# A fused attention and Fourier-mix kernel: turning the exponentials on TensorE instead of by DMA, and moving one cast in GpSimd's order

## The chip, the cores and the metric

The kernel runs on one core of one Trainium2 chip. The metric is the device time of one execution in microseconds (us); lower is better. Times are medians over several executions, and one execution of each kernel is also recorded by the hardware profiler, with every instruction's start, duration and releaser. The engines are named as the profile names them: PE is TensorE's matmul and PEld its weight load, DVE is VectorE, ACT is ScalarE, POOL is GpSimd and SP is SyncE, which here only issues DMAs.

## The reference

For each of 8 batches, 8 heads of a 512-row input `x` and a 32-row `state` attend to each other in both directions; the two results are joined to 544 rows of 512 columns. A Fourier transform over rows and columns is added (real part), the rows are normalised, and a two-layer network with a relu is added.

```python
scores  = (x @ state^T) / sqrt(64);   xread = softmax(scores)  @ state     # 512 rows per head
scores2 = (state @ x^T) / sqrt(64);   sread = softmax(scores2) @ x         #  32 rows per head
a = concat([xread, sread], rows)      # per batch, heads side by side: 544 x 512
u = a + real(fft(fft(a, rows), columns))
un = (u - mean(u)) / sqrt(var(u) + 1e-6)
out = u + relu(un @ w_ch1) @ w_ch2    # w_ch1: 512 x 2048, w_ch2: 2048 x 512
```

## The kernel before

Everything is written for one core, with the order of the instructions of all five engines set by the order in which the Python code emits them. Nothing is rescheduled: each engine works through its own list from top to bottom and waits where an operand is not there. So the place of a step in the code is its place on every engine that it uses.

**Rows.** The 512 rows of a batch lie in four tiles of 128 partitions. Tile 0 is rows 1 to 128; tile 1 rows 144 to 271; tile 2 rows 273 to 400; tile 3 holds 32 single rows (129 to 143, 0, 401 to 415, 272; these are the "low rows") and rows 416 to 511. The transform uses the symmetry of sines and cosines: rows k and 544 - k are added and subtracted ("folded") before they are multiplied with the tables, so tiles 1 and 3 are needed in reverse row order (`XR`), tiles 0 and 2 in forward order (`XF`).

**Steps of one batch `b`.** `load_x` (L115) brings x into `xs` in float32, eight DMAs from SP; `cast_x` (L139) makes the bf16 copy `xin` on GpSimd, one instruction (L140). `turn_state` and `turn_x` (L367, L378) give the transposed `sT` and `xT`; from batch 2 on they are six DMA transposes issued by SP. `scores` (L419) multiplies them on TensorE and writes the exponentials `E` through ScalarE (L430). `E` must then be turned as well, to `ET`, to serve as weights of `xread` (L453). There are two ways in the code. `turn_scores` (L433) multiplies `E` by an identity, or by `mirror` where a tile must be reversed, on TensorE, and ScalarE copies the product to `ET` and adds up the row `sums` (L438); batch 2 takes this way. From batch `e_by_dma = 3` on, `turn_scores_by_dma` (L441) issues two DMA transposes from SP, and `add_scores` (L444) makes the sums by a ScalarE pass over `ET` (L447). [...] for these batches tiles 1 and 3 must be reversed ahead: `turn_x_in_dram` (L134) copies their rows of `x` in reverse order to `x_dram`, two DMAs from memory to memory, one batch ahead, and `load_x` reads `x_dram` for these two tiles.

**Reading and folding.** `read_low` (L511) runs `xread` for tile 3 (TensorE L462, then VectorE L470 and L471 into `XR`), and GpSimd copies its 32 low rows to `XT` (L513). `fold_low` (L515) adds and subtracts halves of `XT` into `XEl` and `XOl` (L516 to L518), on GpSimd too. `sread` (batches 0 and 1) or `sread_by_head` (later batches) overwrites those low rows of `XR` with sread's result (L490 and L492, or L508). For batch 1 GpSimd then adds up a row tile (L529) and makes `XQl` (L523 to L526). `fold` (L537) does the rest on VectorE.

**Transform and network.** `transform` multiplies with the row tables (L634), then with the column tables (L588, L589); VectorE adds (L593) and takes statistics (L330, L332); `ub` is the centred tile, turned to `unT` (by SP's DMA transposes from batch 2 on, L667). `layer1` multiplies `unT` with `w_ch1` (L763 for batch 0, L753 for others; relu on ScalarE, L765 and L755), and `layer2` multiplies with `w_ch2` (L817), scales and adds on VectorE (L784) and stores (L788, L798, L799).

**The order.** Around the start, a list written out by hand (L856 to L860) interleaves transform and first layer of batch 0 with the turns, scores and reads of batch 1. In that list `last_loads` ends with batch 2's cast, `turned[2]` issues batch 2's six transposes and `load_x3` the loads of batch 3. After it, a loop (L865) weaves the streams of neighbouring batches: second layer of `b - 1`, first layer of `b`, reads and transform of `b + 1`, scores of `b + 2`. `warm` fills TensorE with matmuls whose result is not used. PSUM tiles of `scores`, `turn_scores`, `second_axis` and `over_s` share three banks (`psQ`); those of the layers share three others (`psF`); `x2` has one pair.

Of the kernel before, what the change touches and what calls it, by code (L numbers as in the profile page):

```python
# [12 lines left out]
F32 = mybir.dt.float32  # L13
BF16 = mybir.dt.bfloat16
I32 = mybir.dt.int32
AF = mybir.ActivationFunctionType
# [14 lines left out]
def kernel(  # L31
# [8 lines left out]
    nc = tc.nc  # L40
    B, H, S, D = x.shape
    Ns = state.shape[2]
    dm = H * D
# [7 lines left out]

    r_dram = nc.dram_tensor("r_dram", (B, 2, 128, dm), F32, kind="Internal")
    s_dram = nc.dram_tensor("s_dram", (B, H, Ns, D), F32, kind="Internal")
    x_dram = nc.dram_tensor("x_dram", (B, 224, dm), F32, kind="Internal")
# [58 lines left out]
    e_by_dma = 3  # L113

    def load_x(b):  # L115
        xs = wk.tile([128, 4 * dm], F32, name="xs", tag="xs")
        xs_of[b] = xs
        v = xs.rearrange("p (i h d) -> p i h d", i=4, d=D)
        xb = x[b].rearrange("h s d -> s h d")
        back = [x_dram[b, rows].rearrange("r (h d) -> r h d", d=D) for rows in (slice(0, 128), slice(128, 224))]  # L120
        for ps, si, rows in (
            (slice(0, 128), 0, xb[1:129]),
            (slice(0, 128), 1, xb[144:272] if b < e_by_dma else back[0]),
            (slice(0, 128), 2, xb[273:401]),
            (slice(32, 128), 3, xb[416:512] if b < e_by_dma else back[1]),
            (slice(0, 15), 3, xb[129:144]),
            (slice(16, 31), 3, xb[401:416]),
            (slice(15, 16), 3, xb[0:1]),
            (slice(31, 32), 3, xb[272:273]),
        ):  # L130
            queue = nc.scalar if b == 0 and si in (0, 2) else nc.sync
            queue.dma_start(out=v[ps, si], in_=rows)

    def turn_x_in_dram(b):  # L134
        for rows, top in ((slice(0, 128), 271), (slice(128, 224), 511)):
            n = rows.stop - rows.start
            nc.sync.dma_start(out=x_dram[b, rows].rearrange("r (h d) -> h r d", d=D), in_=x[b, :, top:top - n:-1, :])

    def cast_x(b, copy=nc.gpsimd.tensor_copy, lo=0, hi=4):  # L139
        copy(xin_bufs[b % 2][:, lo:hi, 1:513], xs_of[b].rearrange("p (i c) -> p i c", i=4)[:, lo:hi])  # L140
# [163 lines left out]
    def more_loads():  # L304
        state_blocks(1, 2, nc.gpsimd.tensor_copy)
        nc.gpsimd.tensor_copy(gate[:, 0:1], XQ0[:, 3, 0, 0:1])
        cast_x(1)
        nc.gpsimd.tensor_tensor(gate, xs_of[0][:, 0:4], w1[:, :, 3 * 512], op=ALU.add)
        turn_in_dram(3, B)
        load_x(2)  # L310
        turn_x_in_dram(3)
        clears(1)
        nc.gpsimd.memset(stb[:, 2:].rearrange("p b g c -> p (b g c)").bitcast(F32), 0.0)

    def last_loads():
        nc.gpsimd.tensor_copy(gate[:, 0:1], xs_of[2][:, 0:1])
        for q in range(4):
            nc.gpsimd.dma_start(out=w2[:, q * 4:(q + 1) * 4, :], in_=w2v[:, q * 4:(q + 1) * 4, :])
        state_blocks(2, 3, nc.gpsimd.tensor_copy)
        cast_x(2)  # L320

    def qt(name, dt=F32):
        return psQ.tile([128, 512 if dt == F32 else 1024], dt, name=name, tag="q")
# [29 lines left out]
    def attend(b):  # L353
# [8 lines left out]
        ET = wk.tile([128, 2, S] if b < e_by_dma else [128, 8, 128], BF16, name="ET", tag="ET")  # L362
        E = wk.tile([128, 4, 2, 128], BF16, name="E", tag="E")
        sums = wk.tile([128, 2], F32, name="sums", tag="sums")
        Sm = wk.tile([128, 2, 514], BF16, name="Sm", tag="Sm", bufs=1)
# [72 lines left out]
            nc.scalar.activation(ET[:, g, :], p, AF.Copy, accum_out=sums[:, g:g + 1])  # L438


        def turn_scores_by_dma(i):  # L441
            nc.sync.dma_start_transpose(out=ET[:, 4 * i:4 * i + 4, :], in_=E[:, 2 * i:2 * i + 2].rearrange("p a b c -> p (a b c)"))

        def add_scores():  # L444
            junk = Sm[:, 0, 0:512].rearrange("p (a c) -> p a c", c=128)
            for g in range(2):
                nc.scalar.activation(junk, ET[:, g:8:2, :], AF.Copy, accum_out=sums[:, g:g + 1])  # L447

        def weights_of(g, c0):
            return ET[:, g, c0:c0 + 128] if b < e_by_dma else ET[:, c0 // 64 + g, :]  # L450


        def xread(c0, rev, name, o, ps=slice(0, 128), apart=False):  # L453
            n = ps.stop - ps.start
            p = None if apart else x2(name)
            rs = wk.tile([128, 2, 4], F32, name="rs", tag="rs", bufs=4)
            ov = o.rearrange("p (g h d) -> p g h d", g=2, d=D)
            for half in range(2):
                g = 1 - half if rev else half
                rhs = sb[:, g, 259::-1] if rev else sb[:, g, 4:264]  # L460
                ph = psF.tile([128, 512], F32, name=name, tag="c") if apart else p[:, half]
                nc.tensor.matmul(ph[:, 0:260], lhsT=weights_of(g, c0), rhs=rhs, start=True, stop=True)  # L462
# [8 lines left out]
            nc.vector.tensor_tensor(  # L471
                ov, in0=p[ps, :, 0:256].rearrange("p g (h d) -> p g h d", d=D),
                in1=rs[ps].unsqueeze(3).to_broadcast([n, 2, 4, D]), op=ALU.mult)
# [84 lines left out]
        if b < 2:  # L558
            first = [turn_state, lambda: turn_x(0), lambda: turn_x(1)]
            if b == 1:  # L560
                first = [turn_all] + [lambda i=i: copies[i]() for i in range(3)]
            first += [lambda: scores_t(0), lambda: scores_t(1),
                     lambda: scores(0), lambda: scores(1)]
        else:
            first = [lambda: scores(0), lambda: scores(1), lambda: turn_scores(1), lambda: turn_scores(0)]
            if b >= e_by_dma:
                first = [lambda: (scores(0), turn_scores_by_dma(0)), lambda: (scores(1), turn_scores_by_dma(1)), None, None]
            if b >= x_by_dma:
                turned[b] = lambda: (turn_state(), turn_x(0), turn_x(1))
            else:  # L570
                first = [turn_state, lambda: turn_x(0), lambda: turn_x(1)] + first
        read = lambda c0, rev, o: lambda: xread(c0, rev, "xrp" if rev else "xfp", o, apart=(b == 0 and not rev))
        if b < 2:
            second = [read_low, sread, fold_low, read(0, False, XF[:, 0, 0:512]),
                      lambda: (fold_rows(slice(0, 1), nc.gpsimd), fold_low_again()),
                      read(128, False, XF[:, 1, 0:512]), None,
                      lambda: (read(256, True, XR[:, 1, 1:513])(), fold())]
        else:
            second = [read_low, fold_low, read(0, False, XF[:, 0, 0:512]), lambda: (b >= e_by_dma and add_scores(), sread_by_head()),
                      read(128, False, XF[:, 1, 0:512]), None,  # L580
                      lambda: (read(256, True, XR[:, 1, 1:513])(), fold())]
        return first, second
# [256 lines left out]
    def warmed(steps, n):  # L839
        return [lambda s=s: (s(), warm(n)) for s in steps if s is not None]  # L840
# [5 lines left out]
    for step in warmed(s0[:1], 8) + warmed(s0[1:2], 6) + warmed(s0[2:3], 14) + [second_table] + warmed(s0[3:5], 4) + s0[5:]:  # L846
# [1 line left out]
    sin_table()  # L848
    weave((warmed(r0, 4), 0, 1), ([sines], 0.25, 0.25), ([more_sines], 0.3, 0.3),
          ([lambda: warm(44)], 1, 1))  # L850
    load_x3 = lambda: (load_state(3, B, s_dram), load_x(3), turn_x_in_dram(4))
    scores_next, reads_after = attend(2)
    L, M, r1, t1 = layer1(0), layer2(0), reads_next, transform(1)
    W = lambda n: (lambda: warm(n))
    turns1, copies1, s1 = s1[0], s1[1:4], s1[4:]
    for step in (warmed(t0[:2], 2) + [alternate, more_loads] + warmed(t0[2:4], 2) + [exp_again, last_loads, turned[2], load_x3,  # L856
            t0[4], t0[8], W(6), turns1, t0[5], W(10), t0[7], copies1[0], copies1[1], t0[6], copies1[2],
            L[0], s1[0], t0[9], L[1], t0[10], s1[1], L[2], t0[11], t0[12], L[3], s1[2], r1[0], L[4], s1[3],
            r1[2], t0[13], L[5], r1[1], L[6], r1[3], L[7], r1[4], r1[5], L[8], r1[7],
            lambda: state_ones(2, B), lambda: [r() for r in first_roots], L[9], L[10]]):  # L860
        step()
    weave((L[11:], 0, 0.25), (t1, 0.2, 1), ([M[i] for i in (0, 4, 1, 5, 2, 6, 3, 7, 8, 9)], 0.33, 0.99),
# [2 lines left out]
    for b in range(1, B + 1):  # L865
# [10 lines left out]
            streams.append(([lambda: (cast_x(b + 2), turned[b + 2]())], 0.2, 0.2))  # L876
            streams.append((scores_next, 0.5, 1))
        if b + 3 < B:
            streams.append(([lambda: (load_x(b + 3), b + 4 < B and turn_x_in_dram(b + 4))], 0.35, 0.35))
        if b in (3, 7):  # L880
            streams.append((low_rows(b // 4), 0.02, 0.2))
            streams.append((layer1(("L", b // 4)), 0.36, 0.8))
# [31 lines left out]
```

## Time and profile before

| | us |
|---|---|
| median of three runs | 312.68 |
| lowest and highest run | 311.18, 313.35 |
| the profiled execution, whole | 312.68 |
| its span, first to last instruction | 310.9 |
| TensorE busy | 290.4 |
| VectorE busy | 180.5 |
| ScalarE busy | 140.5 |
| GpSimd busy | 96.7 |

A line of instructions in the profile reads: line of the kernel, engine, operation, output `<-` inputs, shapes, then count, busy time, mean duration, and the idle time of the engine just before with what ended it. In a timeline a line begins with the start in us from the span's start and the duration. Matmuls overlap, so their durations add up to more than the time that passes; the distance of two starts is what one costs. `PEld` lines are weight loads, which run beside matmuls. The throttle granted TensorE 0.998 of its full clock.

The DMAs of the two parts that the change touches, as the profile lists them for the whole execution: `x_dram<-in_x_dram`, five of 256 KB and five of 192 KB; `xs<-x_dram`, the same; `ET<-E`, ten transposes. All were issued by SP, on the queue that moved 32.33 MB of the 38.47 MB.

### The profile page before, as it was taken

What the parts mean: (1) busy time and instruction counts of PE and PEld (TensorE: products, weight loads), DVE (VectorE), ACT (ScalarE), POOL (GpSimd) and SP (SyncE); (2) the same over time, 40 slices, a digit from 0 to 9 for tenths busy, and PEclk for the clock granted to TensorE, in tenths of its full rate; (3) what the DMA queues carried; (4) which work ended last, traced back from release to release, by engine and by line L of the source; (5) the groups of instructions that cost most, each with busy time, mean ns of one, the idle gap of its engine ahead of it and who ended that gap; (6) DMA issues with size and microseconds to landing.
All of it is one profiled execution on the core that took longest, in us unless ns stands there. A gap on an engine that the chain in (4) does not pass through costs nothing.

```text
span 310.9 us, 5979 instructions
## 1 busy us (share of the span) xinstructions
PE 290.4 (93%) x2276; PEld 165.4 (53%) x2276; DVE 180.5 (58%) x433; ACT 140.5 (45%) x267; POOL 96.7 (31%) x217
## 2 busy tenths in 40 slices
PE   5968979999968999999999999999999999999993
PEld 5866967544524554456644454445444544555442
DVE  7786674867766576781926756584759474000021
ACT  5777755646533443435434444435343542334200
POOL 4888574490253022700306022601340131000000
PEclk9999999999999999999999999999999999999999
DMA  7998983764754975346753574254333023500354
GB/s 166 204 193 196 174 154 75 194 141 106 195 122 114 217 153 144 69 110 171 177 118 89 131 191 119 63 124 86 101 84 69 35 75 90 124 28 33 76 135 103
DMA packets 117546, 38.47 MB, mean 124 GB/s; under 512 B 107582, under 2 KB 111934, under 8 KB 117518
## 3 DMA queue, kind: packets, MB, share of 16 engines
q1 hardware_dynamic: 106798, 32.33, 44.0%
q0 software_dynamic: 4224, 4.19, 8.5%
q10 hardware_dynamic: 6496, 1.57, 2.3%
q8 instruction: 18, 0.29, 0.4%
q14 instruction: 10, 0.08, 0.1%
HBM read 24.71 MB, written 16.32 MB: 132 GB/s over the span
## 4 chain that ended last, share of the span: by engine, by line
PE 76%; DVE 6%; POOL 5%; issue 4%; ACT 4%; DMA 3%; SPq 1%; POOLq 0%; DVEq 0%; ACTq 0%
PE po L817 31%; PE ph L753 29%; PE ph L763 3%; PE gp L634 2%; PE warm L837 2%; DVE XF L471 2%; POOL xin L140 1%; PE xrp L462 1%; PE po L809 1%; DVE XR L508 1%; PE yp L589 1%; PE yp L588 1%; ACT Sm L447 1%; PE esp L425 1%; DMA xT<-xin 1%
## 5 line engine op out<-in xcount | busy, mean ns | idle before, releaser
L817 PE MATMUL po<-w,hT 128*128 128x512 bf16 x496 | 124.2, 379 | 0.0
L755 ACT ACTIVATE hT<-ph 128x512 bf16<-128x512 f32 x112 | 66.8, 597 | 119.8 <-PE ph L753 118.2
L753 PE MATMUL ph<-unT,w 128*128 128x512 bf16 x448 | 113.7, 379 | 1.5 <-issue 1.5
L753 PEld LDWEIGHTS <-w 128*128 128x128 bf16 x576 | 50.8, 98 | 49.6 <-issue 2.0
L817 PEld LDWEIGHTS <-hT 128*128 128x128 bf16 x496 | 47.3, 98 | 47.9
L784 DVE SCALAR_TENSOR_TENSOR ot<-po,rstd,U 128x512 f32<-128x512 f32 (+2 forms) x33 | 24.2, 733 | 49.5 <-PE po L817 47.3
L638 POOL COPY GL<-G 128x128 bf16<-128x128 bf16 x8 | 2.3, 293 | 80.0 <-ACT G L635 80.0
L593 DVE TENSOR_TENSOR U<-yp,XR 128x512 f32<-128x512 f32 x16 | 10.9, 683 | 26.7 <-PE yp L589 26.7
L336 POOL TENSOR_TENSOR rstd<-mv,epst 128x1 f32<-128x1 f32 x34 | 7.9, 231 | 47.0 <-DVE mv L332 47.0
L337 POOL TENSOR_TENSOR rstd<-rstd,mhalf 128x1 f32<-128x1 f32 x34 | 21.2, 623 | 2.7
L330 DVE BATCH_NORM_STATS2 st<-U 128x6 f32<-128x512 f32 x32 | 21.8, 682 | 0.1
L635 ACT CAST G<-gp 128x288 bf16<-128x288 f32 x31 | 14.5, 483 | 7.7 <-PE gp L634 7.7
L140 POOL CAST xin<-xs 128x2048 bf16<-128x2048 f32 (+1 forms) x9 | 14.4, 1605 | 7.1 <-PE ph L763 3.7
L763 PE MATMUL ph<-unT,w 128*128 128x128 bf16 x256 | 16.1, 219 | 0.5 <-ACT unT L674 0.5
L837 PE MATMUL warm<-ident 128*128 128x128 bf16 x144 | 12.8, 241 | 3.7 <-POOL ident masks.py:199 3.6
L763 PEld LDWEIGHTS <-w 128*128 128x128 bf16 x256 | 15.0, 98 | 0.8 <-issue 0.6
L837 PEld LDWEIGHTS <-ident 128*128 128x128 bf16 x144 | 10.7, 110 | 4.1 <-POOL ident masks.py:199 3.6
L662 DVE TENSOR_SCALAR ub<-U,mv 128x512 bf16<-128x512 f32 x24 | 12.3, 514 | 0.9
L462 PEld LDWEIGHTS <-ET 128*128 128x128 bf16 x64 | 5.3, 98 | 13.6 <-DVE XF L471 5.0
L513 POOL COPY XT<-XR 32x514 bf16<-32x514 bf16 x8 | 4.8, 604 | 21.9 <-DVE XR L471 21.9
L471 DVE TENSOR_TENSOR XR<-xrp,rs 128x512 bf16<-128x512 f32 x16 | 11.1, 695 | 0.7
L593 DVE TENSOR_TENSOR U<-yp,XF 128x510 f32<-128x510 f32 x16 | 10.8, 674 | 0.0
(189 smaller groups left out, 363.0 us busy)
## 6 DMA issues: line engine op xcount, KB each, us to landing
xs<-in_x_dram SPq DMA_DIRECT2D x17, 256.0 KB
w<-in_moe_w_ch_dram POOLq DMA_DIRECT2D x8, 512.0 KB, 11.1
out_dram<-ot SPq DMA_DIRECT2D x15, 256.0 KB
r_dram<-ot SPq DMA_DIRECT2D x14, 256.0 KB
out_dram<-r_dram SPq DMA_DIRECT2D x14, 256.0 KB
x_dram<-in_x_dram SPq DMA_DIRECT2D x5, 256.0 KB
xs<-x_dram SPq DMA_DIRECT2D x5, 256.0 KB
x_dram<-in_x_dram SPq DMA_DIRECT2D x5, 192.0 KB
```

Of the source, the lines that this page charges most:

```text
L140: copy(xin_bufs[b % 2][:, lo:hi, 1:513], xs_of[b].rearrange("p (i c) -> p i c", i=4)[:, lo:hi])
L330: nc.vector.bn_stats(st6, u)
L337: nc.gpsimd.tensor_tensor(rstd, rstd, mhalf, op=ALU.pow)
L471: nc.vector.tensor_tensor(ov, in0=p[ps, :, 0:256].rearrange("p g (h d) -> p g h d", d=D), in1=rs[ps].unsqueeze(3).to_broadcast([n, 2, 4, D ...
L593: nc.vector.tensor_add(u.rearrange("p (k r) -> p k r", r=2), p.rearrange("p (r k) -> p k r", r=2)[:, 0:u.shape[1] // 2, :], x.rearrange("p ...
L635: (nc.vector.tensor_copy if b == 0 and j == 3 else nc.scalar.copy)(G[:, j, :].rearrange("p (i q) -> p q i", q=2), p[:, 0:NM].rearrange("p ...
L753: nc.tensor.matmul(ph[:, o:o + n], lhsT=w1[:, c, f * 128:(f + 1) * 128], rhs=un_of[key][:, c, :], start=(c == 0), stop=(c == DC - 1))
L755: nc.scalar.activation(hT[:, per * i:per * i + per, :].rearrange("p a b -> p (a b)"), ph, AF.Relu, scale=-1.0 if key in flipped else 1.0)
L763: nc.tensor.matmul(ph[:, o:o + 128], lhsT=w1[:, c, f * 128:(f + 1) * 128], rhs=un_of[key][:, c, 128 * r:128 * r + 128], start=(c == 0), st ...
L784: nc.vector.scalar_tensor_tensor(ot[:, cols], in0=po_of[i][:, 0:cols.stop - cols.start], scalar=rstd, in1=u[:, cols], op0=ALU.mult, op1=AL ...
L817: nc.tensor.matmul(po_of[i], lhsT=h_of[key][:, f, i * 128:(i + 1) * 128], rhs=w2[:, f, :], start=(f == 0), stop=(f == FC - 1))
L837: nc.tensor.matmul(t[:, 0:128], lhsT=ident, rhs=ident, start=(i == 0), stop=(i == n - 1))
```

## The change

Two things change together.

First, the exponentials of batches 3 to 7 are turned in the way of batch 2: `turn_scores`, two blocks of five matmuls and two ScalarE passes with row sums per batch. `turn_scores_by_dma`, `add_scores`, `x_dram` and `turn_x_in_dram` are gone, and all tiles are loaded from `x` as for batches 0 to 2.

Second, batch 2's `cast_x` leaves `last_loads`, and with `turned[2]` and `load_x3` it is emitted after `r1[2]`, which is batch 1's `fold_low`. On GpSimd this moves one instruction: the cast stood ahead of `XT`'s copy L513 and now stands behind `XOl` (L518), ahead of L529. On SP the order of the transposes and loads among themselves stays as it was, apart from the DMAs that are gone. On TensorE only the new blocks are added; in the loop they stand a few groups of four layer matmuls ahead of the `xread` that uses them: the second block one group ahead for batch 3, two groups ahead for batches 4 to 7. VectorE's order is the same.

```diff
@@ loads
-            (slice(0, 128), 1, xb[144:272] if b < e_by_dma else back[0]),
+            (slice(0, 128), 1, xb[144:272]),
...
-            (slice(32, 128), 3, xb[416:512] if b < e_by_dma else back[1]),
+            (slice(32, 128), 3, xb[416:512]),
...
-    def turn_x_in_dram(b):
-        for rows, top in ((slice(0, 128), 271), (slice(128, 224), 511)):
-            n = rows.stop - rows.start
-            nc.sync.dma_start(out=x_dram[b, rows].rearrange("r (h d) -> h r d", d=D), in_=x[b, :, top:top - n:-1, :])
@@ more_loads, last_loads
-        turn_x_in_dram(3)
...
-        cast_x(2)
@@ attend
-        def turn_scores_by_dma(i):
-            nc.sync.dma_start_transpose(out=ET[:, 4 * i:4 * i + 4, :], in_=E[:, 2 * i:2 * i + 2].rearrange("p a b c -> p (a b c)"))
-
-        def add_scores():
-            junk = Sm[:, 0, 0:512].rearrange("p (a c) -> p a c", c=128)
-            for g in range(2):
-                nc.scalar.activation(junk, ET[:, g:8:2, :], AF.Copy, accum_out=sums[:, g:g + 1])
...
-            if b >= e_by_dma:
-                first = [lambda: (scores(0), turn_scores_by_dma(0)), lambda: (scores(1), turn_scores_by_dma(1)), None, None]
...
-            second = [read_low, fold_low, read(0, False, XF[:, 0, 0:512]), lambda: (b >= e_by_dma and add_scores(), sread_by_head()),
+            second = [read_low, fold_low, read(0, False, XF[:, 0, 0:512]), sread_by_head,
@@ the order
-    load_x3 = lambda: (load_state(3, B, s_dram), load_x(3), turn_x_in_dram(4))
+    load_x3 = lambda: (load_state(3, B, s_dram), load_x(3))
...
-    for step in (warmed(t0[:2], 2) + [alternate, more_loads] + warmed(t0[2:4], 2) + [exp_again, last_loads, turned[2], load_x3,
+    for step in (warmed(t0[:2], 2) + [alternate, more_loads] + warmed(t0[2:4], 2) + [exp_again, last_loads,
...
-            r1[2], t0[13], L[5], r1[1], L[6], r1[3], L[7], r1[4], r1[5], L[8], r1[7],
+            r1[2], lambda: (cast_x(2), turned[2](), load_x3()), t0[13], L[5], r1[1], L[6], r1[3], L[7], r1[4], r1[5], L[8], r1[7],
...
-            streams.append(([lambda: (load_x(b + 3), b + 4 < B and turn_x_in_dram(b + 4))], 0.35, 0.35))
+            streams.append(([lambda: load_x(b + 3)], 0.35, 0.35))
```

More of the change, by code (lines that the diff above doesn't have):

```diff
@@ L53 @@
     s_dram = nc.dram_tensor("s_dram", (B, H, Ns, D), F32, kind="Internal")
-    x_dram = nc.dram_tensor("x_dram", (B, 224, dm), F32, kind="Internal")
     l_dram = nc.dram_tensor("l_dram", (B // 4, 4, NL, dm), F32, kind="Internal")
@@ L112 @@
     xs_of = {}
-    e_by_dma = 3
     def load_x(b):
@@ L119, in load_x @@
         xb = x[b].rearrange("h s d -> s h d")
-        back = [x_dram[b, rows].rearrange("r (h d) -> r h d", d=D) for rows in (slice(0, 128), slice(128, 224))]
         for ps, si, rows in (
             (slice(0, 128), 0, xb[1:129]),
-            (slice(0, 128), 1, xb[144:272] if b < e_by_dma else back[0]),
+            (slice(0, 128), 1, xb[144:272]),
             (slice(0, 128), 2, xb[273:401]),
-            (slice(32, 128), 3, xb[416:512] if b < e_by_dma else back[1]),
+            (slice(32, 128), 3, xb[416:512]),
             (slice(0, 15), 3, xb[129:144]),
@@ L361, in attend @@
         xT = wk.tile([128, 4, S], BF16, name="xT", tag="xT")
-        ET = wk.tile([128, 2, S] if b < e_by_dma else [128, 8, 128], BF16, name="ET", tag="ET")
+        ET = wk.tile([128, 2, S], BF16, name="ET", tag="ET")
         E = wk.tile([128, 4, 2, 128], BF16, name="E", tag="E")
@@ L438, in turn_scores @@
             nc.scalar.activation(ET[:, g, :], p, AF.Copy, accum_out=sums[:, g:g + 1])
-        def turn_scores_by_dma(i):
-            nc.sync.dma_start_transpose(out=ET[:, 4 * i:4 * i + 4, :], in_=E[:, 2 * i:2 * i + 2].rearrange("p a b c -> p (a b c)"))
-        def add_scores():
-            junk = Sm[:, 0, 0:512].rearrange("p (a c) -> p a c", c=128)
-            for g in range(2):
-                nc.scalar.activation(junk, ET[:, g:8:2, :], AF.Copy, accum_out=sums[:, g:g + 1])
-        def weights_of(g, c0):
-            return ET[:, g, c0:c0 + 128] if b < e_by_dma else ET[:, c0 // 64 + g, :]
         def xread(c0, rev, name, o, ps=slice(0, 128), apart=False):
@@ L461, in xread @@
                 ph = psF.tile([128, 512], F32, name=name, tag="c") if apart else p[:, half]
-                nc.tensor.matmul(ph[:, 0:260], lhsT=weights_of(g, c0), rhs=rhs, start=True, stop=True)
+                nc.tensor.matmul(ph[:, 0:260], lhsT=ET[:, g, c0:c0 + 128], rhs=rhs, start=True, stop=True)
                 if apart:
```

## The prediction

> **What bounds the kernel now.** I read the page's busy shares first, then the table of 10 us windows, and then the timelines of TensorE (PE), GpSimd (POOL) and VectorE (DVE) wherever a window shows TensorE short of full.
>
> ```profile
> PE 290.4 (93%) x2276; PEld 165.4 (53%) x2276; DVE 180.5 (58%) x433; ACT 140.5 (45%) x267; POOL 96.7 (31%) x217
> 40.00:50.00 10.00, 8.10 (x138) 7.88 (x139) 8.51 (x25) 6.52 (x14) 8.29 (x16) 1.00 0.63 115
> 80.00:90.00 10.00, 7.58 (x46) 3.68 (x44) 8.24 (x20) 5.11 (x9) 3.18 (x8) 1.00 0.68 162
> 90.00:100.00 10.00, 8.46 (x73) 3.97 (x71) 5.74 (x15) 2.70 (x7) 5.42 (x9) 1.00 0.44 106
> 100.00:110.00 10.00, 10.00 (x67) 5.28 (x66) 5.55 (x13) 5.27 (x11) 0.29 (x1) 1.00 0.78 184
> ```
>
> In a window row the second number after the length is TensorE's busy time. From 100 to 300 us every window reads 10.00 except three of 9.60: there an instruction added to TensorE costs its time, and one added elsewhere costs nothing. Before 100 us there are holes, and only a hole can be filled. TensorE's timeline shows them (start, duration, last bracket the idle time ahead and its releaser):
>
> ```profile
> 38.81 1.06 PE L763 MATMUL ph<-unT,w 128*128 128x128 bf16 x16
> 41.76 0.39 PE L462 MATMUL xfp<-stb,ET 128*128 128x260 bf16 x2 [1.90 <-DVE XF L471]
> 75.46 0.29 PE L425 MATMUL esp<-sT,xT 128*128 128x64 bf16 x4 [0.54 <-DMA xT<-xin]
> 89.41 0.40 PE L462 MATMUL xrp<-stb,ET 128*128 128x260 bf16 x2 [2.42 <-DMA ET<-E]
> 94.61 1.02 PE L753 MATMUL ph<-unT,w 128*128 128x512 bf16 x4 [1.54 <-issue]
> 169.25 0.40 PE L462 MATMUL xrp<-stb,ET 128*128 128x260 bf16 x2 [0.40 <-DVE XF L471]
> ```
>
> The hole of 1.90 us is explained by GpSimd's and VectorE's timelines around it:
>
> ```profile
> 32.04 1.33 POOL L165 CAST stb<-gen 32x128 bf16<-32x128 f32 x4
> 37.03 1.89 POOL L140 CAST xin<-xs 128x2048 bf16<-128x2048 f32 x1 [3.66 <-PE ph L763]
> 38.87 0.61 POOL L513 COPY XT<-XR 32x514 bf16<-32x514 bf16 x1
> ```
> ```profile
> 35.09 0.70 DVE L471 TENSOR_TENSOR XR<-xrp,rs 128x512 bf16<-128x512 f32 x1
> 37.46 0.17 DVE L483 RECIPROCAL rcs<-srp 128x1 f32<-128x1 f32 x1 [0.91 <-PE srp L481]
> 39.51 1.17 DVE L490 TENSOR_SCALAR XR<-srp,rcs 32x64 bf16<-32x64 f32 x4 [1.89 <-POOL XT L513]
> 41.02 0.69 DVE L471 TENSOR_TENSOR XF<-xfp,rs 128x512 bf16<-128x512 f32 x1
> ```
>
> XR is ready at 35.79, but its copy L513 stands behind the cast of batch 2, which sat until 37.03 for its load (the releaser named, TensorE, read that buffer last for batch 0, long before; so I take it to be the load). VectorE's L490 overwrites XR, so it waits for the copy; XF waits behind L490; TensorE waits for XF.
>
> **What the Trainium skill says.** "Trace Analysis", Identifying the Most-Contended Engine, calls matmul busy time a bad measure because pipelined matmuls overlap. The trace agrees: a 128-column matmul shows 219 ns, but five in a row start every 0.05 us, so I price TensorE by the distance of starts. "TensorE: Matmul & The Clock Gate", Step-by-step: one column of the moving operand per cycle, so cost goes with columns; the five starts below agree (0.24 us for 512 columns). "ScalarE: Activation LUTs", What ACT_TABLE_LOAD costs, gives 186 ns + 0.833 ns per element, an estimate of 612 ns for 512; L438 shows 596. "DMA: Bandwidth & Descriptors", Anatomy of one DMA: a semaphore wait is held by the issuing sequencer. SP's timeline agrees: L667 for batch 2 is issued only from 88.29, behind L442 at 84.88, though its first ub was ready at 82.3.
>
> **Part 1: the cast moved on GpSimd.** One L140 (1.89 us) goes from before L513 to after the fold's last instruction L518. The copy then starts at 35.8 instead of 38.87 and ends at 36.4. L490 now waits for rcs instead (37.46 + 0.17 = 37.63), so VectorE's chain starts at 37.63 instead of 39.51: 1.88 us earlier. TensorE's L462 follows at 39.88, just as L763 ends (38.81 + 1.06 = 39.87). **Gain 1.88.** The cast itself begins at 35.8 + 2.06 (copy to end of fold, 38.87 to 40.93 now) = 37.86, 0.83 later, and ends at 39.75. Behind it on GpSimd waits the row sum L529, which itself waits for ScalarE's L492 (ends 42.25 now, 40.37 then): 0.6 us free, and VectorE's L543 leaves a further 1.64 (45.12 less 43.48). So the cast costs nothing unless its data lands after about 40.1; it landed by 37.03.
>
> What moves with it: two transposes of state, four of x, the state load and eight loads of batch 3. They stand in the same order on SP, with nothing moved past them. SP spent 31.04 to 40.14 issuing the two x_dram copies, and reached the x transposes at 48.78. Without these copies x's four can start at the cast's end, 39.75, end issue at 44.8 (1.25 each), and land about 2.5 later (72.90 to 75.42 is this step for batch 3), at 47.3. TensorE asks for them at 53.83 - 1.88 = 51.95: hidden by 4.6 us. The 0.23 wait of their second half goes. Batch 3's loads then start near 44.8 instead of 54.94, and their cast runs at 68.52: hidden.
>
> **Part 2: Exps turned on TensorE for batches 3 to 7.** Added: ten matmuls per batch, in two blocks of five. Batch 2 shows one block:
>
> ```profile
> 58.81 0.22 PE L437 MATMUL eTp<-ident,E 128*128 128x128 bf16 x1
> 58.87 0.22 PE L437 MATMUL eTp<-mirror,E 128*128 128x128 bf16 x1
> 58.92 0.23 PE L437 MATMUL eTp<-ident,E 128*128 128x128 bf16 x2
> 59.01 0.20 PE L437 MATMUL eTp<-mirror,E 128*128 128x96 bf16 x1
> 59.05 0.38 PE L671 MATMUL tp<-ident,ub 128*128 128x128 bf16 x4
> ```
>
> 58.81 to 59.05 is 0.24 us; 2 x 5 x 0.24 = **2.40 us added**, all in the saturated stretch. On ScalarE two L438 (0.596 + 0.204) replace two L447 (0.626 + 0.189): 0.0, on an engine at 45%. SP loses ten L442 (1.2 to 2.0 each) and ten x_dram copies, and loads two row tiles per batch from x in 256 B pieces rather than from x_dram: SP and the queues are not the bound after 100 us, so 0 there.
>
> Removed waits:
> - 0.54 at 75.46. SP reached x's transposes at 71.66, after the x_dram copies (until 62.77) had delayed the store ahead; the cast ended at 70.40. With SP free at the cast's end, 68.3 on the shifted clock, the second transpose lands at 68.3 + 1.24 + 2.52 = 72.1; TensorE asks at 74.92 - 2.11 = 72.8. Gain 0.54.
> - 2.42 at 89.41: no DMA stands there any more. Gain 2.42.
> - 1.54 at 94.61: the last ub is ready at 87.78, and its transpose takes 2.44 from issue (92.17 to 94.61): 90.2. TensorE would ask at 93.07 - 2.42 + 0.48 + 0.3 = 91.4 on the old clock. Gain 1.54, with 1.2 us to spare.
> - three times 0.40 at 169, 201 and 233: VectorE's L508 waited for sums from L447 (1.93 us at 166.75). The sums now come a stage earlier. Gain 1.2.
>
> New waits, not in this trace: L462 follows the second block by one group of four (0.86 us) in batch 3, two later (1.7), and ScalarE must copy in between (0.6). Low bound 0; batch 2 shows 0.3 on the weight load. High bound: two relus ahead (1.2) plus copy and read (0.8), 2.0 per batch. I take 0.3 in all; and 0.3 more for L462 at 91.36, whose VectorE input would lie behind L784 (87.70 to 88.43).
>
> **Sum.** -1.88 - 0.23 - 0.54 - 2.42 - 1.54 - 1.2 + 2.40 + 0.6 = -4.8. The profiled execution took 312.68 with a span of 310.9, and 312.68 is also the median: 312.68 - 4.8 = **307.9 us** (span 306.1). Bounds of the unknowns: no new wait at all, 307.3; 0.5 per batch, 309.8.
>
> **Rivals.**
> - A, waits replaced: with the DMAs gone, TensorE catches up with VectorE's statistics (busy without a pause from 79.44 to 88.43), and half of the 4.50 us between 75 and 95 comes back: 310.1. For it: that busy stretch; against: the 1.2 us to spare.
> - B, slower: the ET copy decides. At L462 TensorE finds ScalarE still behind with relus, up to 2.0 us in each of five batches in place of the 0.3: -4.8 - 0.3 + 10 = +4.9, 317.6. It decides against the change from about 1 us per batch. Against: ScalarE's gaps of 0.3 to 1.1 between relus in 80 to 88 us.
> - C, the move does nothing: if the load lands late or the copy waits for something else, 1.88 is not won: 309.8. Against: L513 starts the moment the cast ends.
>
> **How the numbers follow.** Forecast 0.60, A 0.18, B 0.11, C 0.11. A difference under 1% (3.13 us, so between 309.55 and 315.8) is about what a measurement cannot tell from no change. Faster: 0.55 of the forecast, 0.04 of A, 0.03 of C: 0.62. Slower: 0.10 of B. Same: the rest, 0.28. The range 305.9 to 311.8 takes in forecast, A and C with their run-to-run spread, and leaves out B and the lower tail.
>
> **What would show it.** L513 starting near 36 and the cast after L518; no hole at L462 near 40; L462 of batch 3 without DMA as releaser; windows of 10.00 from about 85; L437 x50 more, and TensorE's last matmul some 4.8 us earlier. Wrong if L462 shows ScalarE's ET or VectorE's XR as releaser with a microsecond or more, if L753 near 90 still waits for unT, or if L529 waits for the cast.

## The result and the profile after

The changed kernel takes **305.16 us** (median of 6 runs, 304.48 to 305.63); the kernel before, beside it on the same chip, 313.01 (311.08 to 314.43). The ratio is 0.976, with an interval of 0.972 to 0.980. The profiled executions have spans of 302.7 and 310.9 us: 8.2 less. Forecast were 4.8 less, 307.9, and a range from 305.9: the sign is right, the size is not. Medians, here and below, are over all executions of a kernel; ratios leave out those that lie more than 1.5% above its fastest.

First the page of the changed kernel: its busy shares, and the share of each engine in the chain of work that ended last; the third line is that chain in the kernel before.

```profile
PE 290.6 (96%) x2326; PEld 166.7 (55%) x2326; DVE 179.5 (59%) x433; ACT 139.5 (46%) x267; POOL 96.6 (32%) x217
PE 87%; DVE 3%; POOL 3%; ACT 3%; SPq 1%; DMA 1%; issue 1%; POOLq 0%; DVEq 0%; ACTq 0%
PE 76%; DVE 6%; POOL 5%; issue 4%; ACT 4%; DMA 3%; SPq 1%; POOLq 0%; DVEq 0%; ACTq 0%
```

TensorE has 50 matmuls more (2276 before), but its busy time stays near 290 us, so it does not show what changed. The chain does: in the kernel before TensorE holds 76% of it, now 87%; waits for the other engines and for DMAs have gone. The table of 10 us windows of the changed kernel says where (length, then busy time of PE, PEld, DVE, ACT and POOL with counts, granted clock, DMA share, GB/s):

```profile
40.00:50.00 10.00, 9.86 (x153) 8.84 (x151) 7.23 (x24) 7.02 (x14) 7.85 (x13) 1.00 1.31 202
80.00:90.00 10.00, 10.00 (x89) 4.88 (x87) 8.90 (x24) 4.75 (x10) 5.83 (x14) 1.00 0.37 93
90.00:100.00 10.00, 10.00 (x55) 4.91 (x54) 7.76 (x17) 3.96 (x8) 1.96 (x2) 1.00 0.42 79
```

8.10, 7.58 and 8.46 became 9.86, 10.00 and 10.00. The two timelines that carried the first part, GpSimd's and TensorE's, now read:

```profile
35.45 0.60 POOL L491 COPY XT<-XR 32x514 bf16<-32x514 bf16 x1 [1.46 <-DVE XR L449]
...
36.90 0.61 POOL L496 TENSOR_TENSOR XOl<-XT 32x255 f32<-32x255 bf16 x1
37.47 1.89 POOL L132 CAST xin<-xs 128x2048 bf16<-128x2048 f32 x1
40.15 1.16 POOL L507 TENSOR_TENSOR Sm<-XF,XR 128x514 bf16<-128x514 bf16 x1 [0.80 <-ACT XR L470]
```
```profile
38.42 1.06 PE L739 MATMUL ph<-unT,w 128*128 128x128 bf16 x16
39.61 0.40 PE L440 MATMUL xfp<-stb,ET 128*128 128x260 bf16 x2
39.85 1.06 PE L739 MATMUL ph<-unT,w 128*128 128x128 bf16 x16
```

The copy (L491, formerly L513) starts as soon as VectorE has written XR, the cast follows the fold, the row sum behind it waits for ScalarE and not for the cast, and the read (L440, formerly L462) has no bracket: the hole of 1.90 us is gone. For the second part, TensorE's timeline at batch 3's second turning block and the read behind it:

```profile
83.32 0.22 PE L427 MATMUL eTp<-ident,E 128*128 128x128 bf16 x1
...
83.56 1.02 PE L729 MATMUL ph<-unT,w 128*128 128x512 bf16 x4
84.42 0.39 PE L440 MATMUL xrp<-stb,ET 128*128 128x260 bf16 x2
```

The block costs 0.24 us from start to start, one group of four follows, and the read comes 0.86 us after it without waiting for ET.

**Where the 8.2 us went.** The starts of the same matmuls in both traces, subtracted, give a ledger. A step appears where a wait goes or an instruction is added. It sets one execution against one, both at nearly the full clock (0.998 and 1.000); the medians lie 7.85 us apart.

| step, at its time in the kernel before | predicted | measured |
|---|---|---|
| start-up | 0 | -0.36 |
| 41.76, cast behind the fold | -1.88 | -1.79 |
| 56.18, xT in time | -0.23 | -0.39, then +0.39 at 60.31 |
| 75.46, xT in time | -0.54 | -0.71 |
| 89.41, no wait for ET's DMA | -2.42 | -2.59 |
| 94.61, unT in time | -1.54 | -1.61 |
| 169, 201, 233, sums earlier | -1.2 | -1.76 |
| ten turning blocks | +2.40 | +2.32 |
| new waits | +0.6 | 0 |
| last matmul | -4.8 | -6.49 |
| from TensorE's end to the span's end | 0 | -1.7 |

### The profile page after: what moved, and what is told of

The parts are those of the page before. It is cut to its first block, busy times and chain, and to the rows that moved or that the text cites. A ratio compares the mean times of both kernels' runs of the same rounds, so it can differ in the third digit from the quotient of the medians.

```text
span 302.7 us, 6048 instructions
## 1 busy us (share of the span) xinstructions
PE 290.6 (96%) x2326; PEld 166.7 (55%) x2326; DVE 179.5 (59%) x433; ACT 139.5 (46%) x267; POOL 96.6 (32%) x217
## 4 chain that ended last, share of the span: by engine, by line
PE 87%; DVE 3%; POOL 3%; ACT 3%; SPq 1%; DMA 1%; issue 1%; POOLq 0%; DVEq 0%; ACTq 0%
PE po L793 36%; PE ph L729 34%; PE ph L739 4%; PE gp L610 3%; PE po L785 1%; SPq L129 1%; PE xrp L440 1%; PE xfp L440 1%; PE yp L565 1%; PE yp L564 1%; PE esp L415 1%; PE eTp L427 1%; POOL xin L132 1%; DMA xs<-in_x_dram 1%; DVE U L569 1%; ACT XR L470 1%
## 5 line engine op out<-in xcount | busy, mean ns | idle before, releaser
L731 ACT ACTIVATE hT<-ph 128x512 bf16<-128x512 f32 x112 | 66.8, 597 | 118.2 <-PE ph L729 116.1
L813 PE MATMUL warm<-ident 128*128 128x128 bf16 x144 | 12.0, 232 | 3.7 <-POOL ident masks.py:199 3.6
L491 POOL COPY XT<-XR 32x514 bf16<-32x514 bf16 x8 | 4.8, 603 | 23.4 <-DVE XR L449 23.1
L813 PEld LDWEIGHTS <-ident 128*128 128x128 bf16 x144 | 9.9, 104 | 4.1 <-POOL ident masks.py:199 3.6
L741 ACT ACTIVATE hT<-ph 128x512 bf16<-128x512 f32 x16 | 9.3, 597 | 3.2 <-PE ph L739 3.1
```

What stands on the lines that cost most here:

```text
L731: nc.scalar.activation(hT[:, per * i:per * i + per, :].rearrange("p a b -> p (a b)"), ph, AF.Relu, scale=-1.0 if key in flipped else 1.0)
L813: nc.tensor.matmul(t[:, 0:128], lhsT=ident, rhs=ident, start=(i == 0), stop=(i == n - 1))
```

## The experiments

In each diff, lines are of the kernel that is named. The kernel before ran beside every group of experiments (medians 312.5 to 313.9).

**The kernel before, unchanged, once more.**

> The kernel before, once more, for a second profile. Theory F (an instruction fetch of TensorE falls into the last store): the fetch stands at a fixed place in TensorE's list, so the second profile again has one 16 KB packet of the instruction queue between 300 and 303 us, the second out_dram<-r_dram is again issued about 5.1 us after its r_dram<-ot, and from TensorE's last matmul to the end of the span it takes again 4.5 to 4.7 us. Rival, chance: the memory was slow in that one execution; this time about 3.0 us, as in the changed kernel. Both: the span is about 311 us, less 1.7 under the rival.

318.05 us, span 316.3. Two things differ from its first trace. Batch 2's loads were issued later (the last at 33.27 in place of 30.36), the cast ran at 40.11 in place of 37.03, and the hole at the read grew to 4.98 us. From late in that hole on, TensorE was granted half its clock for 6.8 us. The end was as in the first trace: 4.8 us from TensorE's end to the span's end.

**Part 1 alone: the kernel before with only the cast moved.**

```diff
-        cast_x(2)
...
-    for step in (warmed(t0[:2], 2) + [alternate, more_loads] + warmed(t0[2:4], 2) + [exp_again, last_loads, turned[2], load_x3,
+    for step in (warmed(t0[:2], 2) + [alternate, more_loads] + warmed(t0[2:4], 2) + [exp_again, last_loads,
...
-            r1[2], t0[13], L[5], r1[1], L[6], r1[3], L[7], r1[4], r1[5], L[8], r1[7],
+            r1[2], lambda: (cast_x(2), turned[2](), load_x3()), t0[13], L[5], r1[1], L[6], r1[3], L[7], r1[4], r1[5], L[8], r1[7],
```

> Only the second part of the change: cast, transposes and loads behind batch 1's fold; the exponentials of batches 3 to 7 still turned by DMA, the copies to x_dram kept. Theory S (each removed wait counts for itself): only the hole of 1.90 us at 41.76 goes, so 1.8 us less than before, about 311.2; the holes near 75, 89 and 94 and the three of 0.4 stay, and TensorE's list is as long as before, so the end keeps its extra 1.7 us. Rival J (the two parts work only together): the earlier start is lost again where the later holes stand, 313 or more.

313.47 us, ratio 0.999 (0.997 to 1.002): nothing. The move works in its place (the copy starts at 35.95, and the read at 40.11 in place of 41.76), but TensorE's timeline shows what came after it:

```profile
55.19 0.41 PE L424 MATMUL esp<-sT,xT 128*128 128x64 bf16 x8 [0.60 <-DMA xT<-xin]
74.08 0.29 PE L424 MATMUL esp<-sT,xT 128*128 128x64 bf16 x4 [0.27 <-DMA xT<-xin]
75.41 0.29 PE L424 MATMUL esp<-sT,xT 128*128 128x64 bf16 x4 [1.05 <-DMA xT<-xin]
90.00 0.40 PE L461 MATMUL xrp<-stb,ET 128*128 128x260 bf16 x2 [3.08 <-DMA ET<-E]
```

TensorE arrives earlier at transfers that do not come earlier. The waits for xT and for ET grow (1.05 where 0.54 stood, 3.08 where 2.42 stood), and after 90 us nothing is left. SP sets these points; it still issues the x_dram copies first:

```profile
31.12 9.18 SPq L137 DMA_DIRECT2D x_dram<-in_x_dram  x2
48.17 5.73 SPq L380 DMA_TRANSPOSE xT<-xin  x4
```

In the changed kernel, without these copies, the same four transposes are issued from 39.38.

**Part 2 alone: the changed kernel with the cast back in `last_loads`,** and `turned[2]` and `load_x3` behind it as before (the second line of the list is put back as well); run twice.

```diff
+        cast_x(2)
...
-    for step in (warmed(t0[:2], 2) + [alternate, more_loads] + warmed(t0[2:4], 2) + [exp_again, last_loads,
+    for step in (warmed(t0[:2], 2) + [alternate, more_loads] + warmed(t0[2:4], 2) + [exp_again, last_loads, turned[2], load_x3,
```

> Only the first part of the change: exponentials of all batches turned on TensorE, no copies to x_dram; cast, transposes and loads where they were. Theory S: all of the gain but the 1.8 us of the cast, so about 6.0 us less than before, near 307.0, with a hole of about 1.9 us at the second xfp of batch 1. Rival J: the 0.7 and 2.6 us of the later holes come only with the earlier start; then 309 or more.

> The changed kernel without the move of the cast (only the Exps turned on TensorE), once more and beside its rivals. If the cast's move is worth what the hole at 41 us shows (1.7 us on TensorE, minus some 0.3 of warm start), the median lies 0.9 to 1.7 us above the changed kernel's 305.1: 306.0 to 306.8. If the move is worth nothing here either, as it was alone, 305.1 within 0.4.

306.15 us (0.977, interval 0.971 to 0.984) and 306.74 (0.981, 0.977 to 0.985), beside 305.12 for the changed kernel. So part 2 brings nearly all, and the cast some 1.0 to 1.6 us on top of it, where it brought nothing by itself. The intervals overlap that of the changed kernel (0.972 to 0.978), but eight of the ten executions, spread from 305.26 to 310.61, lie above all twelve of the changed kernel (304.5 to 305.6), and in the first trace the last matmul starts 1.7 us later. The second profile shows what can happen at the hole that the cast leaves (TensorE's timeline, then its windows of 2 us, where 1.00 or 0.50 is the granted clock):

```profile
42.45 0.40 PE L441 MATMUL xfp<-stb,ET 128*128 128x260 bf16 x2 [2.61 <-DVE XF L450]
```
```profile
44.00:46.00 2.00, 2.00 (x19) 1.88 (x18) 1.41 (x3) 0.53 (x2) 2.00 (x6) 0.50 1.42 157
48.00:50.00 2.00, 2.00 (x40) 2.00 (x37) 1.94 (x7) 1.31 (x3) 1.92 (x4) 1.00 1.29 280
```

At clock 0.50 TensorE starts 19 matmuls in 2 us, at 1.00 it starts 40, and both windows read as fully busy.

**The kernel before with 24 more unused matmuls** (16 at 15 us, 8 at 26 us), to move TensorE's instruction fetches against the last stores.

```diff
-          ([lambda: warm(44)], 1, 1))
+          ([lambda: warm(60)], 1, 1))
...
-            t0[4], t0[8], W(6), turns1, t0[5], W(10), t0[7], copies1[0], copies1[1], t0[6], copies1[2],
+            t0[4], t0[8], W(6), turns1, t0[5], W(18), t0[7], copies1[0], copies1[1], t0[6], copies1[2],
```

> The kernel before with 24 more warm matmuls in two places where TensorE waits anyway (16 ahead of the first row product of batch 0, 8 ahead of its turn), so 48 more instructions in TensorE's list and nothing else. Theory F: the last instruction fetch comes about 5 us earlier, ahead of the last store; the second out_dram<-r_dram is issued about 3.2 us after its r_dram<-ot, and the kernel is 1.3 to 1.9 us faster than before although it does more. Rival, chance: no change, or up to 0.5 us slower.

313.63 us, ratio 0.996 (0.994 to 0.999): by the ratio, added instructions won 0.3 to 2.0 us; the medians, 313.63 and 313.88, show almost nothing of it. The time alone is weak evidence, and the end of the traces says more. ScalarE's queue issues the last two pieces, a store to r_dram and, when it has landed, the copy of it to the result; first the kernel before, then the changed one:

```profile
300.09 0.81 ACTq L798 DMA_DIRECT2D r_dram<-ot  x1
305.16 0.56 ACTq L799 DMA_DIRECT2D out_dram<-r_dram  x1
```
```profile
293.59 0.91 ACTq L774 DMA_DIRECT2D r_dram<-ot  x1
296.76 0.58 ACTq L775 DMA_DIRECT2D out_dram<-r_dram  x1
```

The same store takes 5.07 us in one and 3.17 in the other. The list of DMA queues of the kernel before, for 300.0 to 304.5 us, shows what else was moved (queue, packets, MB, share of 16 engines):

```profile
q10 hardware_dynamic: 2207, 0.52, 54.8%
q8 instruction: 1, 0.02, 2.3%
q1 hardware_dynamic: 19, 0.04, 2.2%
```

In the changed kernel's stretch (293.5 to 297.0) there is no q8 line. In the whole execution q8 moves 18 packets of 16 KB, one for about every 250 of TensorE's 4552 instructions (2276 matmuls and as many weight loads). That they are TensorE's is seen from the run above: 48 more instructions on TensorE alone move the last packet from 1.8 us after the store's issue to 3.7 us before it (302.36 and 306.02). This run's span, 315.4 us, is long by a hole of 5.91 us at 45.82 and half the clock behind it, far from the end. In all fourteen traces (us; "none": no fetch from the store's issue to its last packet):

| run | store issued | its last packet ends | fetch starts | next issued after |
|---|---|---|---|---|
| kernel before | 300.09 | 304.56 | 301.90 | 5.07 |
| the same again | 305.33 | 310.05 | 308.10 | 5.27 |
| part 1 alone | 300.62 | 304.86 | 302.59 | 4.79 |
| no copies (below) | 297.48 | 302.04 | 299.26 | 5.16 |
| early sums (below) | 298.70 | 302.92 | 300.62 | 4.77 |
| 24 unused matmuls more | 306.02 | 309.05 | none | 3.60 |
| turns twice (below) | 296.12 | 298.71 | 298.92 | 3.12 |
| changed, and again | 293.59, 294.05 | 296.26, 296.47 | none | 3.18, 2.94 |
| part 2, and again | 295.33, 297.90 | 298.32, 300.62 | none | 3.49, 3.23 |
| three mixtures (below) | 295.12, 293.59, 294.47 | 298.26, 296.20, 297.18 | none | 3.66, 3.17, 3.20 |

Where the fetch falls among the store's packets, the next piece is issued after 4.8 to 5.3 us, elsewhere after 2.9 to 3.7. From TensorE's end to the span's end pass 4.1 to 4.8 us with it, 3.0 to 3.3 without.

The single packets tell how the fetch holds the store up. In the kernel before, 120 of the store's 128 packets have ended by 302.68. The last eight start from 303.54 on, as the fetch (301.90 to 303.56) ends, and are done at 304.56, 1.88 us behind the 120th; in the changed kernel this step takes 0.20 us. That makes 1.7 of the 1.9 us between 5.07 and 3.17. All five traces with the fetch show this pause of 0.5 to 1.2 us ahead of the last eight packets, ended within 0.02 us of the fetch's end; in the other nine no two successive starts among the 128 lie more than 0.1 us apart. Eight is a sixteenth of 128, and the profile counts 16 DMA engines: it looks as if the fetch sat on one engine and that engine's eight packets queued behind it. The trace doesn't name a packet's engine, so this last step is inferred.

**The kernel before without the copies to x_dram.** Rows of tiles 1 and 3 of batches 3 to 7 are then read in forward order, so part of the result is computed from other rows.

```diff
-            (slice(0, 128), 1, xb[144:272] if b < e_by_dma else back[0]),
+            (slice(0, 128), 1, xb[144:272]),
...
-        turn_x_in_dram(3)
```

> The kernel before without the ten copies to x_dram; the Exps of batches 3 to 7 are still turned by SP's DMA transposes, and the cast stands where it stood. Rows of tiles 1 and 3 of batches 3 to 7 are read from x in forward order, so these rows of the result are computed from other rows than the reference's. Theory S (the copies on SP's queue, not the turning itself, made the holes between 75 and 95 us): the transposes of x, of E and of ub are issued at once, the holes of 0.54, 2.42 and 1.54 us shrink to less than 1 us in sum, TensorE's matmuls from 100 us on start 4 us or more earlier, and the median lies near 309 (ratio 0.985 to 0.990) or lower. Theory T (an E turned by DMA is late however free SP is): the hole ahead of batch 3's read keeps at least 1.5 us, and the gain is under 2.5 us.

309.65 us, ratio 0.989 (0.986 to 0.993). Neither theory fits whole: the time lies where theory S put it, but the holes are not below 1 us in sum, and the matmuls behind 100 us start 2.6 us earlier and not 4; theory T's hole of at least 1.5 us at batch 3's read is not there. TensorE's timeline, and SP's ahead of it:

```profile
86.59 0.39 PE L461 MATMUL xrp<-stb,ET 128*128 128x260 bf16 x2 [0.88 <-DMA ET<-E]
92.00 1.02 PE L752 MATMUL ph<-unT,w 128*128 128x512 bf16 x4 [1.74 <-DMA unT<-ub]
```
```profile
75.66 5.86 SPq L132 DMA_DIRECT2D xs<-in_x_dram  x8
81.63 3.82 SPq L441 DMA_TRANSPOSE ET<-E  x2
85.56 5.12 SPq L666 DMA_TRANSPOSE unT<-ub  x4
```

Without the copies (2.10 us of SP here, before) the wait for xT near 75 is gone and that for ET is 1.5 us shorter. But ET's two transposes still hold SP for 3.82 us, and unT's four stand behind them; measured against TensorE, which is 2.8 us earlier here, they are as late as before. The three holes fell from 4.50 to 2.62 us; the rest goes in the changed kernel alone, where E isn't turned by DMA.

**The kernel before with the sums of batches 3 to 7 right after the low rows' read.**

```diff
-            second = [read_low, fold_low, read(0, False, XF[:, 0, 0:512]), lambda: (b >= e_by_dma and add_scores(), sread_by_head()),
+            second = [lambda: (read_low(), b >= e_by_dma and add_scores()), fold_low, read(0, False, XF[:, 0, 0:512]), sread_by_head,
```

> The kernel before, with the row sums of batches 3 to 7 added up by ScalarE right after the low rows' read and not one stage later; all else stays. Theory: the three waits of 0.40 us for XF (169, 201, 233 us) come from the late sums; they go, each worth 0.6 us as in the other runs, TensorE's last matmul starts 1.2 to 1.8 us earlier against an undisturbed run of the kernel before, ratio about 0.995. Rival: ScalarE is then in the way of relus or of the division, waits of like size appear in other places, and the ratio is 1.000.

310.76 us, ratio 0.995 (0.991 to 0.998). TensorE's timeline at the first of the three waits:

```profile
168.17 1.03 PE L753 MATMUL ph<-unT,w 128*128 128x512 bf16 x4
169.03 0.39 PE L462 MATMUL xrp<-stb,ET 128*128 128x260 bf16 x2
```

The three waits are gone, and the starts step by -0.56, -0.58 and -0.58 us: 1.7 in all, not 3 x 0.40. The reason is in the first line: a group of four lasts 1.03 us in the record, but the next starts 0.86 us after it. The recorded idle time counts from the recorded end, so each wait is worth 0.17 us more than its bracket.

**The changed kernel with each turning matmul of batches 3 to 7 done twice,** and 25 more unused matmuls at 15 us.

```diff
+            if b > 2:
+                for si, o, rhs in ((0, 0, ident), (1, 128, mirror), (2, 256, ident),
+                                   (3, 384, ident[:, 0:32]), (3, 416, mirror[:, 0:96])):
+                    nc.tensor.matmul(p[:, o:o + rhs.shape[1]], lhsT=E[:, si, g, :], rhs=rhs, start=True, stop=True)
...
-          ([lambda: warm(44)], 1, 1))
+          ([lambda: warm(69)], 1, 1))
```

> The changed kernel, with each turning matmul of batches 3 to 7 done twice (50 matmuls more) and 25 more unused matmuls at 15 us, in a stretch where TensorE is idle for 1.2 us. Two theories with their own place in the trace. Turns: TensorE is the bound from 60 us on, so each block costs 0.23 us again, and the last matmul starts 2.3 us later than in the changed kernel (plus up to 0.4 for the unused matmuls). Fetch: with some 150 more instructions TensorE's last instruction fetch falls into the last store to r_dram, which then takes about 5 us and not 3.2 to its follower, and from TensorE's end to the span's end pass 4.7 us and not 3.0. Together 305.1 + 2.3 + 1.7 = 309.1. If the fetch is harmless, 307.4; if the turns were hidden, 306.8.

306.81 us, by chance the figure that was given for hidden turns. The trace shows that they were not hidden: the starts step by 0.22 to 0.24 us at each doubled block, 2.24 us in all, and the last matmul starts 2.53 us later than in the changed kernel's first trace and 2.07 later than in its second. The turns cost what they show. In TensorE's timeline one block starts at 115.36, its double (L431) at 115.59, and the work behind at 115.83:

```profile
115.36 0.22 PE L427 MATMUL eTp<-ident,E 128*128 128x128 bf16 x1
...
115.59 0.22 PE L431 MATMUL eTp<-ident,E 128*128 128x128 bf16 x1
...
115.83 1.02 PE L797 MATMUL po<-w,hT 128*128 128x512 bf16 x4
```

The other half of the expectation missed: the fetch came at 298.92, 0.2 us after the store's last packet, and the store was not delayed. This run therefore doesn't produce the collision.

**The changed kernel again,** and **three mixtures** with some batches turned on TensorE and the last ones by DMA, all with the cast moved, early sums and `warm(60)`.

```diff
-    e_by_dma = 3
+    e_by_dma = 4
...
-        turn_x_in_dram(3)
```

The second and third have 5 and 6 there, and no copies to x_dram for batches that TensorE turns.

> The changed kernel once more, beside the others on the same chip: 305.2 with a spread below 1.5 us; no hole above 0.6 us after 40 us; last instruction fetch near 285 us and the last store some 3.2 us from issue to its follower. If the spread of the kernel before comes from holes followed by a halved clock, this kernel's span is the same as in its first profile within 1 us.

> The best parts put together: the cast moved behind the fold, batch 3's Exps turned on TensorE, batches 4 to 7 still by DMA (with their copies to x_dram), their row sums early, and 16 more unused matmuls at 15 us that move TensorE's last instruction fetch off the last store. Theory: against the changed kernel it saves four batches times 0.46 us of turning matmuls, and no hole comes back as SP has room from 100 us on: 1.9 us below the changed kernel, near 303.3. Rival: with SP's copies back, the transposes of x, E or ub of batches 4 to 7 are late somewhere, or holes stand again between 60 and 100 us: no better than the changed kernel (305 or more).

> The kernel put together before, with batches 3 and 4 turned on TensorE and 5 to 7 by DMA, and no copies to x_dram before batch 5's. Theory: its hole of 2.11 us at 121 us and that of 0.57 at 88 us came from SP's queue, where E's transposes and x_dram's copies stood ahead of unT's; both go, at 0.46 us for one more batch of turning, so it is 2.2 us below its forerunner and 1.3 below the changed kernel: 303.8. Rival: the waits move to later batches (unT near 150 or 180 us), and it is no better than 305.1.

> As the run with two batches turned on TensorE, now three (3, 4 and 5); only 6 and 7 by DMA, and x_dram is first copied for batch 6, near 103 us. Theory: the hole of 1.21 us at 89 us, where unT stood behind x_dram(5)'s copies on SP, goes, for 0.46 us of turning: TensorE's last matmul starts 0.7 to 0.8 us earlier than there, 304.0. Rival: another transfer is late there or near 120 us in its place, and it is 304.7 or more.

The changed kernel gave 305.12 us (304.8 to 305.43; 0.975, 0.972 to 0.978), its span 303.1, both as expected. With one batch (3) on TensorE, expected near 303.3: 306.02. With two, expected 303.8: 304.73 (0.975, 0.972 to 0.977). With three, expected 304.0: 304.56 (0.974, 0.970 to 0.979). One timeline line of TensorE from each of the three, and SP's ahead of the first:

```profile
121.36 1.04 PE L751 MATMUL ph<-unT,w 128*128 128x512 bf16 x4 [2.11 <-DMA unT<-ub]
```
```profile
110.07 2.56 SPq L440 DMA_TRANSPOSE ET<-E  x2
112.73 0.53 SPq L786 DMA_DIRECT2D out_dram<-ot  x1
113.35 5.14 SPq L665 DMA_TRANSPOSE unT<-ub  x4
```
```profile
89.38 1.02 PE L751 MATMUL ph<-unT,w 128*128 128x512 bf16 x4 [1.21 <-DMA unT<-ub]
```
```profile
120.56 1.02 PE L751 MATMUL ph<-unT,w 128*128 128x512 bf16 x4 [0.92 <-DMA unT<-ub]
```

Each block saved on TensorE gives its 0.23 us, and each time unT is late somewhere: the rivals' mechanism, at 121, at 89 and again at 121 us. In the first, ET's transposes stand ahead of unT's on SP; in the second, batch 5's copies to x_dram (2.00 us from 79.81; unT's first is issued at 82.43); in the third, batch 6's copies (1.95 us from 106.71) and three stores stand ahead of unT's first, issued at 112.90 where the changed kernel has 111.05; that these copies alone make the wait was not tested. The last two stand 0.4 and 0.6 us below the changed kernel, with intervals that overlap its own: no difference that these runs establish, the less so as their 16 unused matmuls alone may be worth this much (last section).

## Why the prediction fell short

- **The cast (-1.88, measured -1.79).** The working holds line by line: L513 near 36, the cast behind L518, L490 released by rcs, the row sum not delayed. What the sum did not say is that this gain needs the other part. Alone it was lost again in four later waits, as SP's transfers did not come earlier. Rival C gave this part no gain; it has none alone, but not for C's reason.
- **0.23 at 56.18.** It went, and came back as a new wait for ScalarE's ub (60.31 in the kernel before, 58.16 here), which rival A's mechanism fits, though A named VectorE: TensorE had caught up with an engine that feeds it.

```profile
58.16 0.40 PE L647 MATMUL tp<-ident,ub 128*128 128x128 bf16 x4 [0.30 <-ACT ub L636]
```

- **0.54, 2.42, 1.54.** All three went, as argued from SP's queue. One reading on the way was off: L667 behind L442 at 84.88 is no case of a wait for a semaphore. The E that L442 turns was written by 81.39 (ScalarE's L430 starts at 80.80 and takes 0.59), and SP reached L442 only at 84.88, behind loads and copies. It shows SP's order, and the argument needs no more. Leaving out the copies alone took these holes from 4.50 to 2.62 us, so both things that were taken from SP count.
- **Turning, +2.40.** Right: +2.32, and doubling the blocks charged them again. TensorE is the bound from 60 us on, and 0.24 per block is a price that can be read from batch 2.
- **New waits, +0.6.** The first mis-sized term: 0. The low bound was the right one. One group of four (0.86 us) is time enough for ScalarE's copy, and rival B's premise, relus in the way, never held TensorE up. The read near 91.36 was not delayed by L784 either.
- **The waits were priced by their brackets.** The second mis-sized term. The prediction priced added matmuls by the distance of starts, and removed waits by the idle time from a modelled end. The Trainium skill, "Perfetto Trace Analysis", Summary: the profiler window per engine type, says that TensorE's recorded end is an estimate; here a group recorded at 1.03 us is followed after 0.86. That is 0.17 a wait: -1.76 for the three waits priced at 1.2, and -0.17 at 75.46 and at 89.41.
- **No term for the end of the trace.** 312.68 - 4.8 carries all that lies around the listed steps over unchanged. The third and largest: from TensorE's end to the span's end pass 3.0 us and not 4.7. A fetch of TensorE's instructions had fallen into the last store; with 50 matmuls more, the last fetch is at 285.0 us, ahead of that store. That fetch and slow store go together is seen in fourteen traces, packet by packet in the five with it, and one experiment moved the fetch and brought the store's 5.07 us to 3.60; its gain in the time (0.3 to 2.0 us) includes whatever the unused matmuls did early on, which was not separated.

Together: 0.6 + 0.7 (brackets and smaller terms) + 0.36 (start-up, whose cause is not settled; the changed kernel's own two traces differ there by 0.46) + 1.7 = 3.4 us, which is 8.2 less 4.8.

## What to carry to other kernels

Where holes stand one behind another, a gain in an early one counts only if the later ones are set by something that moves with it: ask of each later wait what ends it, and whether that comes earlier too. Price a removed wait by what separates the starts around it, less what separates them where nothing waits, not by the idle time in the bracket. And look at the end of the trace as a stage of its own: the last stores can be long for a reason that any change in the number of instructions moves.

## What the runs showed of the hardware

- **An instruction fetch delays a store.** One packet of 16 KB, lasting 0.9 to 1.8 us in the five cases. If it falls among the 128 packets of 2 KB of the last store, the last eight of them wait for its end, and the store takes 4.2 to 4.7 us to its last packet and not 2.4 to 3.1.
- **Half the clock after a hole.** After holes of 4.98 and 5.91 us TensorE was granted 0.50 for 6.8 us; after those of 1.91, 2.14, 2.15, 2.61, 3.00 and 3.08 for 3.4 us; after others of 1.90, 2.11 and 2.42 not at all. The Trainium skill, "TensorE: Matmul & The Clock Gate", What's actually happening, puts the halving after an idle window of about 3.4 us; here a shorter hole was sometimes enough. A hole that is near this length thus costs an uncertain amount. Once two short gaps were enough: in part 2's first trace 3.4 us at 0.50 begin at 21.30, behind gaps of 1.19 and 0.79 us that end at 19.13 and 20.16; the changed kernel's first trace has 1.17 and 0.79 there, without the halving.
- **The mean clock goes with the time.** Of 81 executions of the kernel before, run beside the experiments, the six with a mean granted clock of 0.997 or more took 311.0 to 313.0 us, the twelve with 0.984 or less 314.0 to 317.3. The changed kernel is not free of it: nine of its twelve executions have a mean clock of 0.994, which one period of 3.4 us at half speed gives (an estimate: 0.5 x 3.41 / 303 = 0.006), and took 304.9 to 305.6; the three at 0.999 or more, both profiled ones among them, took 304.5 to 304.9. With 25 unused matmuls more at 15 us all six executions have 1.000; with 16 more, in the three mixtures, fifteen of seventeen have 0.998 or more. That the holes make the wider spread of the kernel before was not tested by itself.
